# A GpSimd copy that reads the last value load, ahead of the weight tiles for raw q and k memory, in a windowed-attention and spectral-mixing kernel

## Chip, cores and metric

The kernel runs on one core of one Trainium2 chip. The metric is device time in microseconds of one launch. A launch takes all inputs from device memory (HBM) and writes one float32 output of 8 x 576 x 512.

## The reference, cut to what matters

Two operators follow each other. The first is causal attention in a window of 128 positions with a linear distance penalty per head (8 batches, 8 heads, 576 positions, 64 channels per head). The second transforms the 576 positions of each batch to frequencies, keeps 64 modes, multiplies each mode with its own complex 512 x 512 matrix, transforms back, adds the input, and applies a channel matrix with a ReLU and a residual.

```python
scores = scale * q @ k.T - slope[h] * |i - j|      # only 0 <= i - j < 128
attn = softmax(scores)
x = (attn @ v)                                      # to [8, 576, 512]
X = np.fft.rfft(x, axis=1)[:, :64]                  # Xr, Xi
Yr = einsum('bmd,mde->bme', Xr, w_r) - einsum('bmd,mde->bme', Xi, w_i)
Yi = einsum('bmd,mde->bme', Xr, w_i) + einsum('bmd,mde->bme', Xi, w_r)
y = np.fft.irfft(Y, n=576, axis=1)
u = x + y
out = u + np.maximum(u @ w_ch, 0.0)
```

The mode matrices are the bulk of the data: 2 x 64 matrices of 512 x 512 in float32, 1 MB each in HBM, against 9.4 MB each for q, k and v.

## The kernel before

**Units and stages.** Attention is cut into 16 units: a batch `b` and a group `g` of four heads. The table `STAGE` (line 38) lists, for one stage, the steps to write out and, with each, a lag: in stage `s` a step with lag `l` works on unit `s - l`. So in stage 13 the query cast (lag -3) has run out of units, the key cast (lag -2) works on unit 15, the value cast (lag 0) on unit 13, and the second half of the value product (lag 1) on unit 12. The order of the instructions on every engine is the order in which this loop (lines 544 to 559) writes them; nothing is moved by a scheduler. `n` is 16, so `n - 3` is stage 13.

**Loads.** `load` (line 201) issues the loads of a unit from SP, and `cast` (line 228) calls it at its end for the unit two further on, since the raw memory of q, k and v has two buffers each. A q or k load is one transfer of 576 KB. A value load is five: one for each head with 512 tokens (line 211, 128 KB each), and one for the last 64 tokens of all four heads (line 215, 64 KB, to partitions 64 to 95). The loads of the last unit, 15, are issued at the end of the value cast in stage 13. VectorE then casts the values to bfloat16 into `vb` (line 236) and `vt` (line 238).

**Weights.** GpSimd issues all weight loads; its transfers turn float32 in HBM into bfloat16 in memory, so a matrix arrives as a tile of 128 x 4 x 512, 512 KB. The order of the matrices is fixed (`todo_w`). During attention they come from two places in the loop. `AHEAD` loads one tile in each of the stages 1 to 13 into the pool `early`; ahead of each, a copy of a single element of `x` (line 556, the "gate") makes GpSimd wait until the attention output of the stage before has been written. `LATER` loads into memory that attention has done with: `spare` (line 439) lists the two buffers of raw q, the two of raw k, and three pieces of raw v. One such tile is loaded in stage 12, and two in each of the stages 13, 14 and 15. In the profile these appear as transfers into `qr`, `kr` and `vr` at line 462, and the ones into `early` as transfers into `w`. After attention, `load_packs` (line 465) loads two matrices at a time into `w` tiles of 1 MB (line 481), as TensorE gives buffers free.

**Two queues.** The 16 DMA engines serve both SP's queue (q1, "hardware_dynamic" in the profile) and GpSimd's (q0, "software_dynamic").

**The spectral part.** From the end of attention on, TensorE multiplies the modes in the fixed order of the weights (line 861), for quads of four modes, with the channel projection of the tokens written in between. After the last quad come the transposes of line 937, and then the remaining channel and token work with the output.

The lines around the change:

```python
            if stage in AHEAD:
                if stage:
                    b, g = at.units[stage - 1]
                    nc.gpsimd.tensor_copy(gate[:1, :1], x[:1, b, 0, 256 * g : 256 * g + 1])
                load_w(AHEAD[stage], early)
            if stage in LATER:
                load_w(LATER[stage], None)
```

Of the kernel before, what the change touches and what calls it, by code (L numbers as in the profile page):

```python
# [71 lines left out]
def _forward_table(nc, pool, F, S):  # L72


    NM = F.shape[2] // 2
    tok = pool.tile([P, FULL + 1], I32)
    nc.gpsimd.iota(tok[:, :FULL], [[P, FULL]], base=0, channel_multiplier=1)
    for bb in range(2):
        nc.gpsimd.iota(
            tok[64 * bb : 64 * bb + 64, FULL : FULL + 1], [[0, 1]],  # L80
            base=FULL * P, channel_multiplier=1,
        )
    mode = pool.tile([P, NM], I32)
    nc.gpsimd.iota(mode, [[1, NM]], base=0, channel_multiplier=0)
    prod = pool.tile([P, FULL + 1, NM], FP32)
    nc.vector.tensor_tensor(
        out=prod,
        in0=tok.unsqueeze(-1).broadcast_to([P, FULL + 1, NM]),
        in1=mode.unsqueeze(1).broadcast_to([P, FULL + 1, NM]),
        op=ALU.mult,  # L90
    )
    turn = pool.tile([P, FULL + 1, NM, 2], FP32)
    for ri in range(2):
        nc.vector.tensor_scalar(turn[:, :, :, ri], prod, float(S) / (4 - 2 * ri), 1.0 / S,
                                op0=ALU.add, op1=ALU.mult)
    whole = pool.tile([P, FULL + 1, NM, 2], FP32)
    nc.vector.tensor_scalar(whole, turn, MAGIC, MAGIC, op0=ALU.add, op1=ALU.subtract)
    nc.vector.tensor_tensor(out=turn, in0=turn, in1=whole, op=ALU.subtract)
    nc.scalar.activation(F[:, : FULL + 1].rearrange("p a b -> p (a b)"),
                         turn.rearrange("p a b c -> p (a b c)"), AF.Sin, scale=TWO_PI)  # L100
    yield
    nc.gpsimd.memset(F[:64, FULL + 1], 0.0)
    nc.gpsimd.tensor_copy(F[64:, FULL + 1], F[64:, FULL])
    nc.gpsimd.memset(F[64:, FULL], 0.0)
# [298 lines left out]
def kernel(  # L403
# [10 lines left out]
    nc = tc.nc  # L414
# [14 lines left out]
    gate = const.tile([P, 8], BF16, name="gate")  # L429
# [7 lines left out]
    raw = {w: rawpool.tile([P, 2, 2, TPP, D], FP32, name=w + "r") for w in "qk"}  # L437
# [15 lines left out]
    def load_w(n, pool, chosen=None):  # L453

        for i in ([i for i in todo_w if i not in again][:n] if chosen is None else chosen):
            todo_w.remove(i)
            src = (moe_w_r, moe_w_i)[i % 2][i // 2].rearrange("(p a) e -> p a e", a=4)
            homes[i] = pool
            t = spare.pop(0) if pool is None else pool.tile([P, 4, DM], BF16, tag="w", name="w")
            for part in ((slice(0, 4),) if i < 2 * NM - 1  # L460
                         else (slice(0, 2), slice(2, 3), slice(3, 4))):
                nc.gpsimd.dma_start(out=t[:, part], in_=src[:, part])
            wq[i] = [t[:, a] for a in range(4)]
# [27 lines left out]
    with ExitStack() as actx:  # L491
        at = _Attention(tc, actx, q, k, v, (ident, F, FT), x, XC, raw)
        n = len(at.units)
        for w, u in (("q", 0), ("k", 0), ("q", 1), ("k", 1), ("v", 0), ("v", 1)):
            at.load(w, u)
        done = set()

        def run(name, arg, u):
            if 0 <= u < n and (name, arg, u) not in done:
                done.add((name, arg, u))  # L500
                getattr(at, name)(u, arg)

        make_identity(nc, ident)
        pool = _Scratch(x[:, B - 2 :].rearrange("p b t c -> p (b t c)").bitcast(FP32))
        wt = at.ps.tile([P, P], FP32, tag="av", bufs=1, name="warm")
        for _ in range(24):
            nc.tensor.matmul(wt, lhsT=ident, rhs=ident, start=True, stop=True)
        table = _forward_table(nc, pool, F, S)
        next(table)
        nc.vector.memset(norm, 2.0 / S)  # L510
        nc.vector.memset(norm[:32], 1.0 / S)
        for t in at.qkT:
            nc.vector.memset(t[:, 1, :, S:], 0.0)
        at.distances(pool)
        at.fixtures(0)
        load_w(1, early)
        next(table, None)
        at.fixtures(1)
        nc.gpsimd.memset(XC[:, 4 * NC * NM :], 0.0)
        run("cast", "q", 0)  # L520
        run("transpose", "q", 0)
        run("cast", "k", 0)
        run("transpose", "k", 0)
        run("evacuate", "q", 0)
        for h in (1, 3):
            at.decay(h)
        run("evacuate", "k", 0)
        run("score", 1, 0)
        for h in (0, 2, 1, 3):
            at.offset(h)  # L530
        run("cast", "q", 1)
        run("transpose", "q", 1)
        run("evacuate", "q", 1)
        run("score", 0, 0)
        run("exp", 1, 0)
        for h in (0, 2):
            at.decay(h)
        run("exp", 0, 0)
        run("cast", "k", 1)
        run("cast", "v", 0)  # L540
        side = {0: [(at.offset, 4), (at.offset, 6), (at.decay, 5), (at.offset, 5), (at.decay, 7),
                    (at.offset, 7), (at.decay, 4), (at.decay, 6)]}
        lags = [lag for _, _, lag in STAGE]
        for stage in range(min(lags), n + max(lags)):
            for name, arg, lag in STAGE:
                run(name, arg, stage - lag)
                if name in ("transpose", "exp") and side.get(stage):
                    for _ in range(1 + (name == "transpose")):
                        fn, h = side[stage].pop(0)
                        fn(h)  # L550
            if stage == 3:
                at.inverse_table()
            if stage in AHEAD:
                if stage:
                    b, g = at.units[stage - 1]
                    nc.gpsimd.tensor_copy(gate[:1, :1], x[:1, b, 0, 256 * g : 256 * g + 1])  # L556
                load_w(AHEAD[stage], early)
            if stage in LATER:
                load_w(LATER[stage], None)

# [441 lines left out]
```

## Time and profile before

| what | value |
|---|---|
| median of 3 runs | 444.19 us (438.96 to 445.89) |
| the profiled execution | 441.24 us, span 439.4 us |
| TensorE matmuls busy | 320.6 us, 73% of the span |
| VectorE, ScalarE, GpSimd busy | 183.7, 162.1, 87.0 us |
| mean granted TensorE clock | 0.847 |
| DMA, GpSimd's queue q0 | 67.22 MB, 76.5% of 16 engines' span |
| DMA, SP's queue q1 | 37.79 MB, 26.3% |
| attention, from the start to the first mode product | 140.76 us |

How to read it: a time is counted from the start of the span. A line of the timeline gives start, duration, engine, source line, operation and operands, the count of merged instructions, and in brackets the idle time ahead with what ended it. "DMA share" is the mean busy share of the 16 DMA engines; it goes somewhat above 1 where packets overlap. A DMA's landing is counted from the start of its issue. The profile is of one execution, so durations are compared with that execution's own time.

### The profile page before, as it was taken

What the parts mean: (1) busy time and instruction counts of PE and PEld (TensorE: products, weight loads), DVE (VectorE), ACT (ScalarE), POOL (GpSimd) and SP (SyncE); (2) the same over time, 40 slices, a digit from 0 to 9 for tenths busy, and PEclk for the clock granted to TensorE, in tenths of its full rate; (3) what the DMA queues carried; (4) which work ended last, traced back from release to release, by engine and by line L of the source; (5) the groups of instructions that cost most, each with busy time, mean ns of one, the idle gap of its engine ahead of it and who ended that gap; (6) DMA issues with size and microseconds to landing.
All of it is one profiled execution on the core that took longest, in us unless ns stands there. A gap on an engine that the chain in (4) does not pass through costs nothing. (4 is left out here: it accounts for less than half of the span.)

```text
span 439.4 us, 8314 instructions
## 1 busy us (share of the span) xinstructions
PE 320.6 (73%) x3509; PEld 177.6 (40%) x3509; DVE 183.7 (42%) x332; ACT 162.1 (37%) x211; POOL 87.0 (20%) x162
## 2 busy tenths in 40 slices
PE   4679899969796724553443387999889999698982
PEld 3357577647665411111111133444444444233430
DVE  7689699788783301010000022332222232122684
ACT  6769799987781000000000012323232323101780
POOL 8611011100323101322113111111111110012500
PEclk8679899999999965555555569999999999989997
DMA  8999999999999999999999999999999999997598
GB/s 280 306 329 301 300 292 312 266 302 283 266 224 213 216 214 213 214 213 214 214 213 215 214 214 214 214 215 215 214 214 215 216 213 214 214 215 135 199 368 306
DMA packets 52489, 105.54 MB, mean 240 GB/s; under 512 B 4052, under 2 KB 23396, under 8 KB 52452
## 3 DMA queue, kind: packets, MB, share of 16 engines
q0 software_dynamic: 18992, 67.22, 76.5%
q1 hardware_dynamic: 33460, 37.79, 26.3%
q8 instruction: 27, 0.44, 0.4%
q14 instruction: 10, 0.08, 0.0%
HBM read 162.53 MB, written 9.44 MB: 391 GB/s over the span
## 5 line engine op out<-in xcount | busy, mean ns | idle before, releaser
L861 PE MATMUL acc<-w,XC 128*32 128x512 bf16 x456 | 80.8, 485 | 68.8 <-DMA w<-in_moe_w_i_dram 35.4
L861 PEld LDWEIGHTS <-XC 128*32 128x32 bf16 x508 | 38.7, 148 | 110.1 <-issue 85.0
L297 ACT ACTIVATE att<-sc 128x1024 bf16<-128x1024 f32 x64 | 64.0, 1031 | 10.0 <-PE sc L287 10.0
L627 ACT CAST ZW<-zw 128x512 bf16<-128x512 f32 x8 | 4.7, 586 | 144.7 <-PE zw L625 144.7
L334 PE MATMUL av<-vb,att 128*128 128x132 bf16 (+1 forms) x576 | 38.4, 217 | 11.6 <-DVE x L350 8.8
L599 DVE TENSOR_SCALAR yq<-acc 128x512 bf16<-128x512 f32 x14 | 9.6, 687 | 82.2 <-PE acc L861 82.2
L334 PEld LDWEIGHTS <-att 128*128 128x128 bf16 x704 | 36.6, 98 | 17.2 <-DVE x L350 13.0
L693 PE MATMUL my<-wch,xT 128*64 128x512 bf16 x288 | 34.5, 381 | 5.8 <-ACT x L724 4.3
L702 ACT CAST XW<-my 128x512 bf16<-128x512 f32 x36 | 19.3, 589 | 50.5 <-PE my L650 50.5
L674 DVE COPY xT<-tr 128x1024 bf16<-128x1024 bf16 x18 | 12.5, 692 | 55.0 <-PE tr L672 55.0
L259 ACT COPY qkT<-tp 128x1152 bf16<-128x1152 bf16 x30 | 33.5, 1115 | 5.3 <-PE tp L253 4.5
L481 POOL DMA_DIRECT2D w<-in_moe_w_i_dram x23 | 16.3, 710 | 66.9 <-PE acc L861 44.2
L481 POOL DMA_DIRECT2D w<-in_moe_w_r_dram x22 | 15.6, 709 | 68.5 <-PE acc L861 48.1
L287 PE MATMUL sc<-qkT 64*64 64x256 bf16 (+2 forms) x640 | 25.7, 269 | 2.5 <-ACT qkT L259 1.6
L350 DVE TENSOR_TENSOR x<-av,rec 128x640 bf16<-128x640 f32 x32 | 26.4, 825 | 1.1
L693 PEld LDWEIGHTS <-xT 128*64 128x64 bf16 x288 | 17.1, 109 | 21.6 <-issue 9.2
L817 DVE TENSOR_TENSOR o<-yy,r 128x1024 f32<-128x1024 f32 (+1 forms) x22 | 21.5, 1025 | 4.8 <-DMA Z<-yq 2.6
L236 DVE CAST vb<-vr 64x1024 bf16<-64x1024 f32 x32 | 22.7, 708 | 0.4 <-DMA vr<-in_v_dram 0.2
L287 PEld LDWEIGHTS <-qkT 64*64 64x64 bf16 x640 | 14.8, 110 | 19.8 <-issue 16.5
L556 POOL COPY gate<-x 1x1 bf16<-1x1 bf16 x13 | 5.5, 423 | 86.2 <-DVE x L350 86.2
L724 ACT CAST x<-my 128x512 bf16<-128x512 f32 x18 | 10.6, 586 | 31.0 <-PE my L650 31.0
L274 PE MATMUL sc<-bias,ident 128*128 128x512 bf16 x64 | 20.7, 408 | 1.1 <-ACT att L297 1.1
(134 smaller groups left out, 431.0 us busy)
## 6 DMA issues: line engine op xcount, KB each, us to landing
w<-in_moe_w_i_dram POOLq DMA_DIRECT2D x23, 1024.0 KB, 35.8
w<-in_moe_w_r_dram POOLq DMA_DIRECT2D x22, 1024.0 KB, 35.7
qr<-in_q_dram SPq DMA_DIRECT2D x16, 576.0 KB, 9.2
kr<-in_k_dram SPq DMA_DIRECT2D x16, 576.0 KB, 8.2
vr<-in_v_dram SPq DMA_DIRECT2D x64, 128.0 KB, 7.6
w<-in_moe_w_r_dram POOLq DMA_DIRECT2D x16, 512.0 KB, 14.3
w<-in_moe_w_i_dram POOLq DMA_DIRECT2D x13, 512.0 KB, 24.0
out_dram<-o SPq DMA_DIRECT2D x13, 512.0 KB, 4.6
```

The lines of the kernel that those rows point to most:

```text
L236: nc.vector.tensor_copy(self.vb[u % 2][row, :, :, :, W * half : W * half + D], src[row, :2])
L259: (self.nc.vector.tensor_copy if u < 2 and w == "q" else self.nc.scalar.copy)(dst.rearrange("q h (p j) -> q h p j", j=TPP), tp.rearrange(" ...
L274: nc.tensor.matmul(sc[:, e], lhsT=self.ident, rhs=self.bias[:, hv].rearrange("p j n -> p (j n)"), start=True, stop=False, skip_group_check ...
L287: nc.tensor.matmul(sc[64 * half : 64 * half + 64, e, j * 256 + c0 : j * 256 + c0 + n], lhsT=qkT[row, 1, h, k0 + j : k0 + P : 2], rhs=qkT[r ...
L297: self.nc.scalar.activation(self.att[u % 2][:, kt * 8 * P : (kt + 1) * 8 * P], sc.rearrange("p e n -> p (e n)"), AF.Exp, scale=1.0 / math. ...
L334: nc.tensor.matmul(bank[:, qt * W : qt * W + rhs[j].shape[1]], lhsT=att[:, o : o + P], rhs=rhs[j], start=(n == 0 and j == 0), stop=(n == l ...
L350: nc.vector.tensor_tensor(out=self.x[:, b, :, cs].rearrange("p t (h d) -> p h t d", h=2), in0=tiles[:, :, :, :D], in1=rec.unsqueeze(-1).br ...
L481: nc.gpsimd.dma_start(out=t.rearrange("p s a e -> p s (a e)"), in_=w[kinds.pop()][m : m + 2].rearrange("m (p a) e -> p m (a e)", a=4))
L693: nc.tensor.matmul(mm[ROWS[half]], lhsT=lhsT, rhs=wch[:, dt], start=(dt == 0), stop=False, skip_group_check=True,)
L702: nc.scalar.copy(XW[:, j, n], mms[n])
L817: nc.vector.tensor_tensor(out=o[:, c], in0=yy[:, c], in1=r[:, c], op=ALU.add)
L861: nc.tensor.matmul(into[32 * (m % 4) : 32 * (m % 4) + 32], lhsT=XC[:, c0 : c0 + 31 * NM + 1 : NM], rhs=wq[t][a], start=(ri == 0 and a == 0 ...
```

## The change

Behind the `AHEAD` tile of stage 13 and ahead of the two `LATER` tiles of that stage, GpSimd copies four elements of the raw value buffer with index 1, the one of unit 15, into `gate`: partition 0, second half of the 512 tokens, the four heads, channel 0. Each of the four is written by another of the four head transfers of unit 15. The copy is therefore released when those four have landed. The fifth transfer, with the last 64 tokens, is not read. Nothing else is changed.

```diff
@@ -555,6 +555,8 @@
                     b, g = at.units[stage - 1]
                     nc.gpsimd.tensor_copy(gate[:1, :1], x[:1, b, 0, 256 * g : 256 * g + 1])
                 load_w(AHEAD[stage], early)
+            if stage == n - 3:
+                nc.gpsimd.tensor_copy(gate[:1, :4], raw["v"][:1, (n - 1) % 2, 1, :, 0])
             if stage in LATER:
                 load_w(LATER[stage], None)
```

## Prediction

> **What bounds the kernel now.** I read the page's slices first, then the busy time by stretches, the waits of the spectral part, and last, close up around 116 to 130 us, GpSimd's order of time, SP's, and the DMA queues.
>
> The slices and the queue table of the page:
>
> ```profile
> DMA  8999999999999999999999999999999999997598
> q0 software_dynamic: 18992, 67.22, 76.5%
> q1 hardware_dynamic: 33460, 37.79, 26.3%
> ```
>
> The 16 DMA engines are busy from the first slice to about 400 us. Queue q0 is what GpSimd issues, the 64 + 64 weight matrices in tiles of 512 KB; q1 is what SP issues, the q, k and v loads and the output. Two of the 50 us stretches (columns: length, PE, PEld, DVE, ACT, POOL, granted clock, DMA share, GB/s):
>
> ```profile
> 150.00:200.00 50.00, 22.55 (x116) 8.82 (x109) 4.32 (x18) 0.00 (x0) 9.58 (x15) 0.58 1.06 214
> 350.00:400.00 50.00, 43.05 (x297) 19.09 (x295) 13.08 (x23) 10.12 (x19) 5.35 (x10) 0.97 1.06 214
> ```
>
> The share and the rate are the same in all five stretches from 150 to 400, while TensorE's busy time and clock change by a factor of two. One tile takes 524288 B / 214 GB/s = 2.45 us there. The waits of 150 to 400 us say who suffers:
>
> ```profile
> PE acc L861 <- DMA w<-in_moe_w_i_dram: 35.2, 16, 5.1
> PE acc L861 <- DMA w<-in_moe_w_r_dram: 31.7, 15, 3.9
> ```
>
> So the weight stream sets the time of everything up to its last landing (issued at 390.37, landing 14.9 us later, 405.3); the chain that ended last starts with the transposes at 406.38 and runs 33 us after that. An instant in which the DMA engines stand idle before 400 us is never won back: the stream has one length, and the end moves by the idle time. Attention is off this path by a little: it hands over at 140.76, TensorE runs on tiles already there to about 152.8, and then waits 3.39 us, to 156.21, for the first double tile.
>
> **What the change touches.** GpSimd and SP in order of time, before (start, duration):
>
> ```profile
> 118.27 0.51 POOL L556 COPY gate<-x 1x1 bf16<-1x1 bf16 x1 [6.78 <-DVE x L350]
> 118.72 0.53 POOL L462 DMA_DIRECT2D w<-in_moe_w_i_dram  x1
> 119.24 0.54 POOL L462 DMA_DIRECT2D qr<-in_moe_w_r_dram  x1
> 119.76 0.55 POOL L462 DMA_DIRECT2D kr<-in_moe_w_r_dram  x1
> 120.28 0.56 POOL L462 DMA_DIRECT2D kr<-in_moe_w_i_dram  x1
> 123.47 0.54 POOL L462 DMA_DIRECT2D vr<-in_moe_w_i_dram  x1 [2.64 <-DMA vr<-in_v_dram]
> 129.35 1.06 POOL L462 DMA_DIRECT2D vr<-in_moe_w_r_dram  x2 [5.34 <-DVE vb L236]
> ```
>
> ```profile
> 116.05 2.34 SPq L211 DMA_DIRECT2D vr<-in_v_dram  x4
> 121.04 0.33 SPq L215 DMA_DIRECT2D vr<-in_v_dram  x1
> ```
>
> This is stage 13. The tile of 118.72 (into `w`) stays where it is. The new copy stands behind it and ahead of the tiles of 119.24 and 119.76; the next stage's two, at 120.28 and 123.47, are queued behind them on GpSimd and move too. Nothing else is on GpSimd until 129.35. The copy reads the four head transfers of the last unit, which SP issued at 116.05; the fifth, the 64 KB of the last 64 tokens (121.04), goes to other partitions and is not read. **Removed: nothing. Added: one copy and its wait. Moved: four DMA issues.** SP's queue is not passed by anything.
>
> **The gain: zero.** Does a moved tile now hold back the value transfers? Queue lines of the trace, first for 121 to 124.2 us, then for 124 to 127 us (packets, MB, share):
>
> ```profile
> q0 software_dynamic: 135, 0.52, 81.2%
> q1 hardware_dynamic: 483, 0.23, 29.8%
> ...
> q0 software_dynamic: 160, 0.59, 96.4%
> q1 hardware_dynamic: 129, 0.06, 10.1%
> ```
>
> 0.52 MB is just the tile of 118.72, whose first packets come near 120.9. The first moved tile therefore starts at about 124.2, and in 123 to 124 there is no hardware packet left: the heads are through before a moved tile moves a byte. And nobody would use them earlier:
>
> ```profile
> 127.67 1.38 DVE L236 CAST vb<-vr 64x1024 bf16<-64x1024 f32 x2
> ```
>
> VectorE comes to this cast straight from its own work, with no wait. The last head transfer was issued at 117.8 and landed 5.8 us later, 123.6: 4.1 us of cover. The 64 KB transfer landed at 121.04 + 7.0 = 128.04, ahead of its cast at 128.97; it would have to be 0.9 us later to cost anything, and with the queue beside it empty it gets sooner.
>
> **The loss, step by step.** (1) The copy is released at 123.6. From a released gate copy to the DMA issue behind it the rows give 118.72 − 118.27 = 0.45 us (0.45 also at 109.97 and at 102.30). So the first moved tile is issued at 124.05, not 119.24, and the others 0.52 us apart. (2) From issue to the first data. Software tiles that found their queue empty: issued 59.32, first packets just after 60.7 (1.4 us); 118.72, near 120.9 (2.2); 11.38, near 14.1 (2.7); 102.75, near 106.1 (3.4). The last from the trace's 103 to 106 us, where the hardware queue is alone:
>
> ```profile
> q1 hardware_dynamic: 687, 0.98, 108.4%
> ```
>
> Ends 1.4 and 3.4; I take 2.7, near the middle of them and seen beside the busy queue of loads as well. First data at 124.05 + 2.7 = 126.75. (3) The software queue ran dry at 124.2, so it is empty for 126.75 − 124.2 = 2.55 us. (4) The 64 KB of values, 10.1% of 3 us = 0.3 us of the engines' time, now run in the gap and no longer beside weights. Idle: 2.55 − 0.3 = **2.25 us**; with the ends 1.4 and 3.4, 0.95 and 2.95. (5) No second gap: the next tiles are issued at 124.6 and 125.1 and are ready while the first still moves (to 129.2), and the fourth, 125.6 instead of 123.47, is not due before 134. The tiles of 129.35 wait for the VectorE cast as now. (6) The tiles themselves are used by TensorE from 147.5 on and land near 131 to 136, 10 us early; what is late next is the first double tile, 156.2 becoming 158.5, and from there every landing to the last.
>
> The Trainium skill, page "DMA: Bandwidth & Descriptors", section on latency and other measured facts, puts the first byte of a DMA issued by GpSimd at about 1 us. By that the gap would be 124.05 + 1.0 − 124.2 − 0.3 = 0.55 us, and the time 441.8. No tile here started that soon, the measured 1.4 to 3.4 us decide, and nothing below rests on this.
>
> **The sum.** The profiled execution took 441.24 us (span 439.4 and 1.8 around it): 441.24 + 2.25 = 443.5. The median of the three runs is 444.19, 2.95 above that execution, and the runs lie from 438.96 to 445.89; on the median's scale it is 446.4. I predict the middle, 445.0, half a per cent slower and within the 2% which is about what a measurement of this kernel can tell from no change. For the likeliest alone I would give 441 to 449, which is the gap's ends on both scales and the scatter of a few runs.
>
> **Rivals.** *The gap is hidden.* If the stream had slack later, or the value transfers had landed before GpSimd came to the copy, there would be only the copy's 0.45 us, under the tile still moving: 441.2 by the profile, 444.2 by the median. Against it: share 1.06 in every stretch from 150 on, and a landing 5 us after GpSimd reaches the copy. 0.12.
>
> *The copy waits for the fifth transfer too*, if the dependency is kept coarser than the bytes. It landed at 128.04: 128.04 + 0.45 + 2.7 − 124.2 − 0.3 = 6.7 us at most, 447.9 (450.9 by the median). For it: nothing but the shared tile `vr`. Against: the tile of 123.47 goes into the same `vr` and was issued 4.6 us before that landing. 0.06.
>
> *Slower by over 2%: the heads land late.* The page of `vr` has landings up to 12.4 us. At 117.8 + 12.4 = 130.2 the gap would be 130.2 + 0.45 + 2.7 − 124.2 − 0.3 = 8.85 us, 450.1, which is 2.0%; it decides from a landing at 130 us on. Against: the long landings belong to stages in which q and k loads run too, and the last k load was issued at 108.0. 0.08.
>
> *Faster.* Values come sooner and attention ends sooner. The whole wait of the last casts for values is 0.2 us, and the handover at 140.76 is not what the stream waits for; under 1 us, 440.5. 0.04.
>
> **How the numbers follow.** Likeliest 0.70, the rivals as given. Slower by over 2%: half of the late heads with some of the coarse wait, 0.07, and 0.05 for scatter on top of the likeliest: 0.12. Faster by over 2%: 0.04, the faster rival and scatter below the hidden gap. Within 2%: 0.84. Range 439.5 to 450.5: it takes in the hidden gap by the profile's time, the coarse wait nearly whole, and leaves out most of the late heads.
>
> **What would show it.** In the changed profile: a gate copy from `vr` with some 5 us of wait, ending near 123.6; the `qr` tile issued near 124; in 124.5 to 126.5 a DMA share well below 1 with no software packets; the cast of 127.67 unmoved; TensorE's hand-over at 140.8 unmoved, but its wait after 152.8 longer by 2 us; and the last transposes near 408.6. The prediction is wrong if the DMA share shows no hole, if the hole is there and the final transposes do not move, or if the hole is over 5 us.

## The result, and the profile after

The changed kernel takes 441.64 us (median of 22 runs, 439.91 to 444.68), the kernel before 439.36 us (22 runs, 438.23 to 445.89). The ratio is 1.0046, with a 95% interval of 1.0024 to 1.0068: 2.0 us longer (1.1 to 3.0), a small loss that is clear of the noise. The profiled execution of the changed kernel took 441.08 us, span 438.9, so its span is shorter than that of the profile before. The two profiles can't be subtracted as wholes; they have to be read around the change.

GpSimd in order of time, changed kernel (start, duration):

```profile
117.05 0.51 POOL L556 COPY gate<-x 1x1 bf16<-1x1 bf16 x1 [6.63 <-DVE x L350]
117.50 0.53 POOL L462 DMA_DIRECT2D w<-in_moe_w_i_dram  x1
122.96 0.29 POOL L559 CAST gate<-vr 1x4 bf16<-1x4 f32 x1 [4.93 <-DMA vr<-in_v_dram]
123.47 0.54 POOL L462 DMA_DIRECT2D qr<-in_moe_w_r_dram  x1 [0.22 <-DMA vr<-in_v_dram]
123.99 0.54 POOL L462 DMA_DIRECT2D kr<-in_moe_w_r_dram  x1
```

The new copy waits 4.93 us for the value heads (the four head transfers of unit 15). The first moved tile is issued 6.42 us after the gate copy of the stage, where it was 0.97 us after it (118.27 to 119.24). The stretches of the kernel before, and then of the changed kernel (the last two columns are DMA share and GB/s):

```profile
122.00:124.00 2.00, 1.72 (x31) 1.11 (x28) 1.92 (x5) 2.00 (x3) 0.53 (x1) 1.00 1.15 235
124.00:126.00 2.00, 2.00 (x41) 1.48 (x35) 1.82 (x3) 1.52 (x3) 0.01 (x1) 1.00 1.06 216
```

```profile
122.00:124.00 2.00, 1.72 (x22) 1.20 (x22) 1.92 (x5) 2.00 (x3) 0.83 (x3) 1.00 0.50 108
124.00:126.00 2.00, 2.00 (x41) 1.40 (x41) 1.84 (x3) 1.52 (x3) 1.59 (x4) 1.00 0.53 73
...
150.00:200.00 50.00, 21.95 (x116) 8.83 (x109) 4.37 (x19) 0.00 (x0) 9.54 (x15) 0.61 1.06 214
```

There is now a hole of (1.06 − 0.50) x 2 + (1.06 − 0.53) x 2 = 2.18 us. Below, "hole" is always this: what is missing to 1.06, in the 2 us stretches (from even times, behind the gate copy) with a share under 1.00. After it the stream runs at 214 GB/s as before. What comes behind is unmoved in its kind: the cast of the last values still follows VectorE's own work with no wait,

```profile
128.02 1.38 DVE L236 CAST vb<-vr 64x1024 bf16<-64x1024 f32 x2
```

and the chain's final transposes start here, before and after:

```profile
406.38 0.23 PE tr L937 x2
...
406.46 0.22 PE tr L939 x2
```

Why is the end not 2 us later than 406.38? Because the gate copy of this execution is at 117.05 and that of the profile before at 118.27: it came through the attention stages 1.2 us sooner, ahead of any changed instruction. From the gate copy to the final transposes it is 406.46 − 117.05 = 289.4 us after and 406.38 − 118.27 = 288.1 us before. This distance is the number by which all runs below are compared; the attention ahead of it scatters by 2.9 us in the profiles of this case (gate copy at 115.36 to 118.27).

By the same mark the cast of the last values is later, though: 128.02 − 117.05 = 10.97 us after the gate copy, against 127.67 − 118.27 = 9.40 us before. That shift is not the loss. Of the three profiles of the changed kernel two have it (10.97 and 10.84 us) and the third, which lost most, has not (9.41); and the kernel with one tile ahead of the copy, below, has it too (10.70 us) in a profile in which the end is not late at all.

### The profile page after: what moved, and what is told of

Read it like the earlier page. It is cut to its first block, busy times and chain, and to the rows that moved or that the text cites. A ratio compares the mean times of both kernels' runs of the same rounds, so it can differ in the third digit from the quotient of the medians.

```text
span 438.9 us, 8307 instructions
## 1 busy us (share of the span) xinstructions
PE 321.1 (73%) x3509; PEld 179.4 (41%) x3509; DVE 184.5 (42%) x332; ACT 162.0 (37%) x211; POOL 87.7 (20%) x163
## 5 line engine op out<-in xcount | busy, mean ns | idle before, releaser
L334 PE MATMUL av<-vb,att 128*128 128x132 bf16 (+1 forms) x576 | 39.4, 220 | 12.2 <-DVE x L350 7.7
L334 PEld LDWEIGHTS <-att 128*128 128x128 bf16 x704 | 37.6, 100 | 17.8 <-DVE x L350 11.9
L676 DVE COPY xT<-tr 128x1024 bf16<-128x1024 bf16 x18 | 12.4, 692 | 55.6 <-PE tr L674 55.6
```

The source lines that it names most:

```text
L334: nc.tensor.matmul(bank[:, qt * W : qt * W + rhs[j].shape[1]], lhsT=att[:, o : o + P], rhs=rhs[j], start=(n == 0 and j == 0), stop=(n == l ...
```

## The experiments

Theory A: GpSimd's queue of weights runs dry while the copy waits, the DMA engines idle, and nothing later gives that back. Rival B: GpSimd's wait or the read of the values costs in itself. Rival C: the hole is made up later.

### The changed kernel, the copy behind the tiles, one tile ahead, and a bare delay

The changed kernel again:

> The changed kernel once more, as the yardstick for the other runs on the same chip. Theory A (GpSimd's queue of weights runs dry while the copy waits, and the idle of the DMA engines is carried to the end): ratio to before 1.003 to 1.007; in the stretch from 122 to 126 us a DMA share of about 0.5. Rival B (GpSimd's stop itself costs, through what it issues later or through what it takes from other engines): the same ratio, and nothing here tells the two apart. Rival C (the profiled pair is right, which ends its final transposes at 406.38 and 406.46, and the hole is made up later): 0.999 to 1.002.

Measured: 1.0044 (1.0011 to 1.0078). In its profile the copy is released 5.5 us after the gate copy, the hole is 1.34 us, and the distance 289.2 us. The loss is repeated; a hole that later work makes up (C) would not leave it.

The copy behind the two tiles:

```diff
             if stage in LATER:
                 load_w(LATER[stage], None)
+            if stage == n - 3:
+                nc.gpsimd.tensor_copy(gate[:1, :4], raw["v"][:1, (n - 1) % 2, 1, :, 0])
```

> The same copy with the same wait, but behind the two weight tiles of that stage instead of ahead of them. GpSimd still stands still until the heads land, near 123.5 us, and the next stage's tiles are still issued after it. Theory A: two tiles are now queued that keep the DMA engines busy to about 129 us, so there is no hole, the DMA share stays at 1.05 or more from 122 to 130, and the ratio to before is 0.998 to 1.002. Rival B: the wait is as long as in the changed kernel, so the ratio is as there, 1.003 to 1.007. Rival C: 0.999 to 1.001, without a hole.

Measured: 1.005 (1.0016 to 1.0085). The ratio is B's and my expectation from A missed it. The profile says why. GpSimd, VectorE and two stretches:

```profile
130.48 0.70 POOL L561 CAST gate<-vr 1x4 bf16<-1x4 f32 x1 [11.75 <-DMA vr<-in_v_dram]
130.45 1.39 DVE L236 CAST vb<-vr 64x1024 bf16<-64x1024 f32 x2 [3.96 <-DMA vr<-in_v_dram]
...
128.00:130.00 2.00, 2.00 (x33) 1.28 (x30) 0.00 (x0) 0.99 (x3) 0.00 (x0) 1.00 0.20 42
130.00:132.00 2.00, 0.64 (x14) 0.26 (x12) 1.53 (x3) 1.81 (x2) 1.52 (x3) 1.00 0.00 1
```

There is a hole after all, later and larger: 4.76 us with the next stretch (0.60). The copy was released at 130.48 and not near 123.5, because the heads took 14.4 to 14.5 us from issue to landing, against some 6 us in the first profile of the kernel before and in the two of the changed one so far. They were issued at the usual time, 2.2 us ahead of the gate copy. The queue lines of this kernel for 124.5 to 129 us, with weights queued, and for 129.2 to 130.2 us, when they had run out (packets, MB, share):

```profile
q0 software_dynamic: 218, 0.77, 85.4%
q1 hardware_dynamic: 24, 0.01, 1.2%
...
q1 hardware_dynamic: 40, 0.02, 6.5%
```

24 packets of the hardware queue got through in 4.5 us beside weights, and 40 in the 1.0 us after. So the rest of the values, in packets of some 0.5 KB (0.23 MB in 483 packets, by the prediction's lines), got on slowly while weight packets of some 4 KB (0.52 MB in 135) were queued, and the last of them landed only once the weights had run out. The kernel before shows the same contrast: from 116 to 117 us, beside a busy weight queue, 51 hardware packets moved with 52 software packets; from 119 to 120 us, when the weight queue had little, it was 533 with 16. Queued weights alone do not make the heads this late, though: in the kernel before four tiles were queued beside them, and they landed after 6 us. The Trainium skill, page "DMA: Bandwidth & Descriptors", section "Queues, rings and completion order", says that each DMA engine takes turns between its queues packet by packet; the even counts of 51 and 52 fit that, but the profile doesn't give packets by engine, so the turn-taking itself is not shown here. What is shown: **waiting for a landing beside queued weights can mean waiting until the weights are gone.** The distance is 292.8 us, 4.7 more than without a hole. A holds for the cost; what was wrong was the release time that I put into it.

One tile ahead of the copy, one behind:

```diff
-            if stage in LATER:
+            if stage == n - 3:
+                load_w(1, None)
+                nc.gpsimd.tensor_copy(gate[:1, :4], raw["v"][:1, (n - 1) % 2, 1, :, 0])
+                load_w(1, None)
+            elif stage in LATER:
                 load_w(LATER[stage], None)
```

> The copy stands between the two weight tiles of the stage: one tile (raw q memory) is issued ahead of it, the other (raw k memory) behind it. Theory A: one tile is 2.45 us of the stream, so the queue runs dry at about 126.7 instead of 124.2; the tile behind the copy is issued near 124 and its data come 1.2 to 2.7 us later, 125.2 to 126.7, so there is no hole or one of a few tenths: ratio 0.998 to 1.002. Rival B: as the changed kernel, 1.003 to 1.007.

Measured: 1.0041 (1.0003 to 1.0079), and in the one profile no hole at all, a release 6.4 us after the gate copy, and a distance of 288.1 us. The 12 runs lie from 438.48 to 444.58, four of them under 440. The profile fits A, the ratio does not, unless in other executions the copy was released late, as in the kernel above; that is argued and not shown, and why this ratio is so high stays open.

A delay with no read of values:

```diff
+            if stage == n - 3:
+                for _ in range(28):
+                    nc.gpsimd.tensor_copy(gate[:1, 4:5], gate[:1, :1])
             if stage in LATER:
                 load_w(LATER[stage], None)
```

> No value is read. In the place of the copy GpSimd does 28 tiny copies within gate, of some 0.18 us each by the gate copies of the profile, so that the two weight tiles are issued about 5 us late, as in the changed kernel, with no wait for any transfer. Theory A: the hole comes from the lateness of the issue alone: a hole of 1.5 to 3 us in the DMA share between 122 and 127 and a ratio of 1.003 to 1.007. If the tiny copies are shorter than 0.18 us, the hole shrinks by as much. A theory that the read of the values or its semaphores cost: 0.998 to 1.002.

Measured: 1.0094 (1.0063 to 1.0125). The copies took longer than the 0.18 us that I had put in:

```profile
117.62 8.45 POOL L560 COPY gate<-gate 1x1 bf16<-1x1 bf16 x28
...
122.00:124.00 2.00, 2.00 (x40) 1.36 (x40) 1.93 (x5) 1.52 (x3) 1.64 (x7) 1.00 0.64 132
124.00:126.00 2.00, 1.49 (x33) 1.26 (x33) 1.75 (x4) 2.00 (x3) 1.64 (x7) 1.00 0.03 8
126.00:128.00 2.00, 2.00 (x44) 1.80 (x40) 1.96 (x5) 1.66 (x2) 1.69 (x4) 1.00 0.16 31
```

That is 0.302 us each, so the tiles were 3.3 us later than in the changed kernel, the hole 4.9 us with the next stretch (0.96), and the distance 292.8 us. No transfer is waited for and no value read, and the cost is twice that of the change: lateness of the issue is enough. The ratio alone, 0.0094 x 439.8 = 4.1 us more, says the same.

### Two more profiles of the kernel before, an earlier landing, and half the delay

The kernel before, twice, for the profile only:

> The kernel before, once more, for a second profile of it: how much of an execution's time is decided ahead of the change. In the profiles so far, the time from the gate copy of stage 13 to the final transposes is 288.1 us before, 289.4 and 289.1 in two profiles of the changed kernel, and 292.7 in the delayed one, while the gate copy itself lies anywhere from 115.7 to 118.3 us. Theory A (idle DMA time after that copy is carried to the end): again 288 us with no hole between 117 and 133 us, whatever the gate copy's own time. A theory that the changed kernel differs ahead of the gate: this number moves with the gate's time.

> As the run ahead of it: a third profile of the kernel before. Theory A: 288 us from the gate copy to the final transposes, if the values of the last unit land before they are needed; if weights come between them and they land late, as in the run with the copy behind the two tiles (heads 14 us from issue to landing), VectorE waits for them, the tiles into raw v memory are issued late, and the number is larger.

The second gave what A expects: no hole, gate copy at 115.36, distance 288.3 us, 438.11 us in all. The first did not: it shows late values in the kernel before. The heads of the last unit from issue to landing, and VectorE's cast of them:

```profile
DMA to landing us min/median/max: 9.1/11.5/13.8
...
129.94 1.39 DVE L236 CAST vb<-vr 64x1024 bf16<-64x1024 f32 x2 [3.69 <-DMA vr<-in_v_dram]
```

Attention's last conversion came 29.3 us after the gate copy, not 21.9. Yet the distance is 289.1 us: being 7 us late with attention cost 1.0 us at the end, with a hole of 0.6 us at 132 to 138 us, where the tiles into raw v memory had to wait for that cast.

The copy reading unit 14, whose heads land sooner:

```diff
+            if stage == n - 3:
+                nc.gpsimd.tensor_copy(gate[:1, :4], raw["v"][:1, (n - 2) % 2, 1, :, 0])
             if stage in LATER:
                 load_w(LATER[stage], None)
```

> The copy at the same place, but it reads the four heads of the unit before, 14, in the other buffer, which in the profile before had landed by 121.8 us, about 2 us ahead of those of unit 15. Theory A, with the hole as the time between the end of the last queued tile and the first data of the next: the tiles are issued near 119.5 to 122 instead of 121.7 to 123.5, the data of the first come 1.2 to 2.7 us later, and the queue runs dry at 122 to 124: a hole of 0 to 1 us, ratio 0.999 to 1.003. A theory that any wait or read of the values at this place costs: 1.003 to 1.007 as in the changed kernel.

Measured: 0.9999 (0.9967 to 1.003). Released 4.1 us after the gate copy (tile at 4.65), hole 0.26 us, distance 288.2 us. The same instruction at the same place, waiting for transfers of the same kind (3.12 us, against 4.93), cost nothing that the runs can show where the queue was fed in time. That is against B.

Half the delay, 14 copies:

> The delay again, half as long: 14 tiny copies, which took 0.302 us each in the run with 28 of them, so 4.2 us, and no wait for a transfer. With 28 the tiles were issued 9 us after the gate copy's tile and the ratio was 1.0094; here they are issued 4.7 us after it, a little before those of the changed kernel (5.6 and 6.0 us). Theory A: a hole of 0.3 to 1.8 us, ratio 1.001 to 1.004. A theory that a stop of GpSimd costs by its length: 1.004 to 1.005, half of the run with 28.

Measured: 0.9998 (0.9974 to 1.0021). The profiled execution has the tile 5.5 us after the gate copy, a hole of 0.82 us and a distance of 289.7 us, 1.6 more than without a hole. The ratio is lower than I expected from A, and lower than that one execution suggests; it would fit if in most of its runs the queue was fed about in time, which is argued and not shown. GpSimd was held up by 4.2 us in the profiled execution, and by the rival's price that should have given 1.004 to 1.005, above the whole interval: the length of the stop is not what is paid.

### Longer and shorter waits

The copy reading the fifth transfer:

```diff
+            if stage == n - 3:
+                nc.gpsimd.tensor_copy(gate[64:65, :4], raw["v"][64:65, (n - 1) % 2, 2, :, 0])
             if stage in LATER:
                 load_w(LATER[stage], None)
```

> The copy at the place of the changed kernel, but it reads the fifth transfer, the 64 KB with the last 64 tokens, instead of the four heads. SP issues it behind the heads, and in the profiles of the changed kernel its last packets came 1 to 2 us after theirs. Theory A: GpSimd is released 1.5 to 2.5 us later than in the changed kernel, the hole is 3 to 4.3 us instead of 1.2 to 2.0, and the ratio 1.006 to 1.010. A theory that the cost is fixed for a wait at this place: 1.003 to 1.007.

Measured: 1.0058 (1.0032 to 1.0085). Released 7.6 us after the gate copy, hole 3.32 us, distance 290.9 us. Release and hole are as A expected. The ratio is just under A's range and inside that of a fixed cost, so by the ratio alone this run does not tell the two apart.

The copy ahead of all three tiles:

```diff
                 if stage:
                     ...
+                if stage == n - 3:
+                    nc.gpsimd.tensor_copy(gate[:1, :4], raw["v"][:1, (n - 1) % 2, 1, :, 0])
                 load_w(AHEAD[stage], early)
```

> The copy of the changed kernel, one tile earlier: ahead of the stage's tile into the pool early as well, so three weight tiles wait for the heads of unit 15 and not two. Theory A: nothing of this stage is queued while GpSimd waits, the queue runs dry about 2.5 us sooner, but the values then have the engines to themselves and land sooner, by up to 2 us: a hole of 1.5 to 4 us, ratio 1.004 to 1.009, and the release nearer to the gate copy than the 5.5 to 5.9 us of the changed kernel. If the landing does not depend on the weights queued ahead, the release stays at 5.5 to 5.9 us and the hole is 4 us or more.

Measured: 1.0057 (1.0028 to 1.0085), hole 3.50 us, distance 291.3 us. It was released 5.5 us after the gate copy, as in the quickest profile of the changed kernel and not sooner: one tile less ahead of the values did not bring them forward. For a landing that comes no sooner I had expected a hole of 4 us or more; it was 3.5.

The copy one stage later:

```diff
             if stage in LATER:
                 load_w(LATER[stage], None)
+            if stage == n - 2:
+                nc.gpsimd.tensor_copy(gate[:1, :4], raw["v"][:1, (n - 1) % 2, 1, :, 0])
```

> The same copy one stage later: behind the two tiles of stage 14, ahead of the two into raw v memory that wait for the cast of these values anyway. Theory A: GpSimd is held by the same transfers, but with four tiles (10 us of the stream) more in the queue, and what stands behind the copy could not be issued earlier in any case: no hole, ratio 0.998 to 1.003, and as in the kernel before some executions longer, in which the values land late. A theory that the wait for these transfers itself costs: 1.003 to 1.007.

Measured: 0.9991 (0.9957 to 1.0025). In its profile the copy ran with no wait: the tile ahead of it had already waited 2.59 us, to 122.90, and by the time of the copy the heads had landed (the last was issued at 117.4 and took 5.7 us). The tiles behind it wait for VectorE as always:

```profile
122.90 0.53 POOL L462 DMA_DIRECT2D vr<-in_moe_w_i_dram  x1 [2.59 <-DMA vr<-in_v_dram]
123.43 0.18 POOL L561 CAST gate<-vr 1x4 bf16<-1x4 f32 x1
128.83 1.10 POOL L462 DMA_DIRECT2D vr<-in_moe_w_r_dram  x2 [5.22 <-DVE vb L236]
```

Reading the values cost nothing here; holding back tiles that keep the engines fed did.

A third profile of the changed kernel:

> A third profile of the changed kernel, to see how much the hole differs between executions. Theory A, from the profiles so far: 287.9 us from the gate copy to the final transposes and the hole on top of that, 1 to 3 us, as long as the heads take from the gate copy to their landing beyond some 4 us.

442.75 us. The heads took 8.8 us to land and the copy was released 8.1 us after the gate copy:

```profile
122.00:124.00 2.00, 2.00 (x41) 1.48 (x35) 1.97 (x4) 1.52 (x3) 0.00 (x0) 1.00 0.42 86
124.00:126.00 2.00, 1.49 (x32) 1.06 (x30) 1.48 (x4) 2.00 (x3) 1.27 (x4) 1.00 0.00 1
```

Hole 3.54 us with the next stretch (0.99), distance 291.8 us: a larger hole than the 1 to 3 us expected, and the end later by as much.

### All profiles in one table

Times in us; "more" is the distance from gate copy to final transposes less 288.1, the mean of the four profiles without a hole (287.8, 288.1, 288.1, 288.3).

| kernel | hole | more | ratio |
|---|---|---|---|
| before (3 profiles) | 0, 0, 0.6 | 0.0, 0.2, 1.0 | 1 |
| one stage later | 0 | −0.3 | 0.9991 |
| one tile ahead | 0 | 0.0 | 1.0041 |
| reads unit 14 | 0.3 | 0.1 | 0.9999 |
| half delay | 0.8 | 1.6 | 0.9998 |
| changed (3 profiles) | 1.3, 2.2, 3.5 | 1.1, 1.3, 3.7 | 1.0046, 1.0044 |
| fifth transfer | 3.3 | 2.8 | 1.0058 |
| ahead of three tiles | 3.5 | 3.2 | 1.0057 |
| behind the tiles | 4.8 | 4.7 | 1.005 |
| full delay | 4.9 | 4.7 | 1.0094 |

The first two number columns agree within 0.9 us over all fourteen profiles, whatever made the hole: a wait, a delay, or values held up by weights. The length of GpSimd's wait does not order the costs. Three profiles have nearly the same one, 4.84 us with one tile ahead, 4.93 us in the first profile of the changed kernel and 4.98 us ahead of three tiles, and cost 0.0, 1.3 and 3.2 us with holes of 0, 2.2 and 3.5 us:

```profile
122.60 0.18 POOL L560 CAST gate<-vr 1x4 bf16<-1x4 f32 x1 [4.84 <-DMA vr<-in_v_dram]
...
121.75 0.53 POOL L558 CAST gate<-vr 1x4 bf16<-1x4 f32 x1 [4.98 <-DMA vr<-in_v_dram]
```

That settles A for the cost, against B and C, in the profiled executions. The ratios are over 9 to 22 runs, whose holes are not known one by one; they follow less closely, and two of them, one tile ahead and half delay, do not fit the hole of their one profile. No kernel here is faster than the one before; the two that come out level with it (unit 14, one stage later) merely do no harm.

## Why the prediction was right or wrong

**The mechanism and its size: right.** "Idle: 2.55 − 0.3 = 2.25 us" stands against holes of 1.3, 2.2 and 3.5 us in three profiles of the changed kernel, mean 2.35, and a loss of 2.0 us by the ratio. The order of the moved tiles, a last cast with no wait for values, and the unmoved rate from 150 us on are as written. Two of the signs that the prediction named did not show as written, since it gave them as times from the start of one execution. The final transposes came at 406.46 and not near 408.6, and by the prediction's own words that would refute it; from the gate copy they are 1.3 us later. TensorE's wait for the first double tile was 3.52 us and not 2 us longer than 3.39, because TensorE too took over later by that mark (24.0 us after the gate copy, against 22.5); the wait ended 39.51 us after the gate copy, against 37.94.

**The terms.** (1) The release was put at 5.3 us after the gate copy (123.6 − 118.27); it was 5.9, 5.5 and 8.1. I took one execution's landing as fixed. The spread of the holes comes from here. (2) For the first data I took 2.7 us with ends 1.4 and 3.4; in the profile after it was about 1.2: these are the queue lines from the issue, 123.47, to 124.6, and for 124.6 to 125 us.

```profile
q0 software_dynamic: 9, 0.02, 11.1%
...
q0 software_dynamic: 5, 0.02, 51.0%
```

The 9 packets are the rest of the tile before; in the second stretch, which is 0.4 us long, the next tile sets in. So a later release and sooner data in part made up for each other, and the 2.25 is partly luck. The 1 us for the first byte that the Trainium skill gives (page "DMA: Bandwidth & Descriptors", latency and other measured facts) is nearer to this one row than my middle; by the earlier rows it was too low.

**The predicted time: wrong by 3.4 us.** 445.0 was against a measured 441.64. The step that failed is the base to which the gap was added: "on the median's scale it is 446.4. I predict the middle, 445.0". The three runs shown had a median of 444.19, but 22 runs of the same kernel have 439.36; two of those three were among its longest. The middle mixed two scales, and it set the number only 0.8 us (0.2%) over the median shown, when the sum's own gap was 2.25 us (0.5%) and the runs gave 2.0. From the profiled execution alone it would have been 443.5; that execution, 441.24, was itself 1.9 us over the later median. As a difference the sum was good to 0.3 us.

**"The gain: zero": right for the time, too simple in its reason.** It rested on one profile in which the heads were through before a moved tile moved a byte. Another profile of the kernel before has them 13.8 us on the way and VectorE waiting 3.69 us. The three profiles of the changed kernel show no wait ahead of this cast. So the change may protect the values, but three profiles of each kernel are too few to show it, and it would be worth no more than the 1.0 us that the late values cost there, less than the hole.

**The rivals.** The hidden gap: no. The fifth transfer: the copy does not wait for it, by the release at 122.96, since the fifth, issued at 120.34, took 4.9 us and landed at 125.2; made to wait for it, the kernel lost 2.8 us and not 6.7. Late heads: landings beyond the 12.4 us of this rival did happen, 14.5 us with the copy behind the two tiles and 13.8 us in the kernel before, but in the changed kernel none over 8.8 us. The sentence that long landings belong to stages with q and k loads was wrong: in both of those profiles the last k load had landed by 114 us. It cost 4.7 us behind the two tiles, since the queue still held weights for a good part of the wait.

## What to carry to other kernels

Where one stream of transfers sets the end, cost an edit by the time for which that stream's queue is empty, and not by how long an engine waits: a copy with the same read cost 0, 1.3 or 4.7 us in its profile, by where it stood and when the values landed. A wait for a landing ahead of the next transfer's issue pays for the landing, the restart of the issuing engine and the time to the next transfer's first data; leave enough queued to cover that, but know that what is queued also holds up the landing. And compare profiles from a fixed mark near the change, since what happens ahead of it scattered here by more than the effect.

## What the runs showed of the hardware

I had not expected small loads to be held up this far by large queued ones: the same four transfers of 128 KB took some 6 us (5.6 to 6.6) from issue to landing in nine of the fourteen profiles, 8.8 to 9.1 in three (the third of the changed kernel, the full delay, and the copy that reads unit 14), and up to 13.8 and 14.5 in two with three or four weight tiles queued beside them. In the last of these the rest of the values got on with 24 packets in 4.5 us beside weights and 40 in 1.0 us without. Four queued tiles were also there in three profiles with 6 us, so they do not decide it alone. What decides, from one execution to the next, whether the values or the weights get there first stays open.
